# A scheduled two-layer recurrent kernel: new durations in its scheduling model, and a new order of all work

## Chip, cores and metric

The kernel runs on one core of a Trainium2 chip. The metric is the device time in microseconds (us); lower is better. Every kernel here ran several times and was compared with the kernel before on the same chip in the same rounds. A difference under 2% counts as "same", so most questions below, which are about 5 to 50 us in 1590, are answered by the intervals and by the traces.

## The reference, cut to what matters

Two memory-augmented attention layers and two gated feed-forward layers alternate. An attention layer goes through 64 segments of 32 rows one after the other; eight memory rows that a segment puts out are read by the next one, so each layer is a chain of 64 steps.

```python
def _A_ref(x, mem0, Wq, Wk, Wv, Wo, seg_len):      # 16 heads of 256, 8 memory rows
    mem = mem0
    for s in range(n_seg):                          # 64 segments of 32 rows
        h = concat([mem, x[:, 32*s : 32*s+32]])     # 40 rows
        p = softmax(mask(q(h) @ k(h).T / 16))
        o = (p @ v(h)) @ Wo
        mem = o[:, :8]                              # the next segment reads this
        outs.append(o[:, 8:])
def _B_ref(x, W_gate, W_up, W_down):                # width 448 -> 1792 -> 448
    return (relu(x @ W_gate) * (x @ W_up)) @ W_down

x = x + _A_ref(_layernorm(x), ...)
x = x + _B_ref(_layernorm(x), ...)
x = x + _A_ref(_layernorm(x), ...)                  # the same weights again
return x + _B_ref(_layernorm(x), ...)
```

## The kernel before

The kernel does not write its instructions in a fixed order. It lists several thousand operations with what they read and write, their engine and a duration in ns, and a greedy list scheduler plays them on model engines. At each point it takes, of the operations that could start about now, the one with the highest priority: the length of the longest chain behind it, plus a constant from a fitted table. The order in which the model starts operations is the order in which the program issues them. **So a duration in the model never changes how long anything takes on the chip. It changes the order alone.**

```python
BIAS = { "": 86257.0, "t_block": 36012.0, ... , "stay": 41740.0 }     # fitted priorities, cut

class _Order:
    LAT = {"pe": 170.0, "act": 0.0, "dve": 0.0, "pool": 60.0, "sp": 2200.0}
    def run(self):
        ...                                    # t: when o could start on engine e (inputs, buffers, engine)
        lim = max(f, t0) + (60.0 if e == "pe" else 40.0)
        stay = BIAS.get("stay", 0.0) if e == "pe" else 0.0
        t, o = max((x for x in lst if x[0] <= lim), key=lambda x: (x[1].prio + stay * (x[1].mode == mode), -x[0]))
        ...
        c = o.cost[e]
        if e == "pe" and o.mode != mode:
            c += 95.0                          # a change of TensorE's tile form
        if e in ("act", "dve"):
            free[e] = t + c - 60.0             # back-to-back work overlaps
        ...
    def emit(self):
        for o in self.order:                   # what the model started first is issued first
            ...

@staticmethod
def acost(n):                                  # ScalarE, n columns
    return 186.0 + n / 1.2

def tdma(self, name, out, src, rd, wr):        # small transposes: xAT, xBT, PTs
    self.q.add("dma", ("sp",), {"sp": 1250.0}, lambda E: E.dma_start_transpose(out=out(), in_=src()), rd, wr, name=name, lat=1150.0)
```

Three operations:

- `xBT`: one DMA transpose for each two segments. It turns the layer-normed rows `xn` for the feed-forward layer, which starts with it. In front of it stand `un` (28 or 56 matmuls with `U`, the tile `big` in the trace) and the layernorm.
- `PTs`: one DMA transpose in each segment. It turns the probabilities `Ps` for the products that give `U`.
- `un_mem` and `m_t`: the chain of the memory. 56 matmuls give the eight rows, ScalarE copies their high half (`hi`), VectorE takes the low half (`lo`), selector matmuls (`selm`) transpose both, VectorE copies the result (`hT`), and the next step can begin.

```python
def un_mem(self, t):
    ...
    S.mm(mms, 14 * S.pitch(D) + 100.0, [("UTm", w, 0), ("UTm", w, 1), ...], C.res() + [("hi",), ("lo",)], mode=2)
    S.act(lambda E: E.activation(S.hi[:, :], C.b()[:, 0:D], ACT.Copy), D, C.res(), [("hi",)])
    S.dve(lambda E: E.tensor_tensor(S.lo[:, :], C.b()[:, 0:D], S.hi[:, :], ALU.subtract), D, C.res() + [("hi",)], [("lo",)])

def ln_b(self, p):
    S.ln(S.XB[:, p % 2, :], ...)
    ...
    S.tdma("xBT", lambda: S.xBT[:, :, :], lambda: S.xn[:, 1, :], [("xn", 1, 0), ("xn", 1, 1)], [("xBT",)])
```

Of the kernel before, what the change touches and what calls it, by code (L numbers as in the profile page):

```python
# [12 lines left out]
D = 448  # L13
# [31 lines left out]
class _Sched:  # L45
# [107 lines left out]
BIAS = {  # L153
    "": 86257.0, "t_block": 36012.0, "t_block@a": 23035.0, "t_block+": -1249.0, "s_mem": 20903.0, "s_mem@a": 89077.0,
    "s_mem+": -30020.0, "p_t_mem": 19749.0, "p_t_mem@a": 43910.0, "p_t_mem+": 2707.0, "u_mem": 55095.0,
    "u_mem@a": -130.0, "u_mem+": -99280.0, "un_mem": -459.0, "un_mem@a": 122.0, "un_mem+": -17548.0, "m_t": 272938.0,
    "m_t@a": -12858.0, "m_t+": 2514.0, "s_seg": -17721.0, "s_seg@a": -110875.0, "s_seg+": -84825.0, "seg_pt+": 2945.0,
    "seg_pt@a": 61065.0, "u_seg": -7984.0, "u_seg@a": -190957.0, "u_seg+": -15770.0, "m_nat": 209021.0,
    "m_nat@a": -66163.0, "m_nat+": -6349.0, "ln_a+": 6133.0, "ln_a@a": -40396.0, "un": -45873.0, "un@a": 985.0,
    "un+": -360.0, "ln_b+": 36834.0, "ln_b@a": -3899.0, "b_layer": -14517.0, "b_layer@a": -4185.0,  # L160
    "b_layer+": -36139.0, "b_down": -43343.0, "b_down@a": 11698.0, "ln_a@1": -121626.0, "ln_a@3": 37724.0,
    "m_nat@0": 28359.0, "t_block@0": -6404.0, "s_mem@0": -40022.0, "p_t_mem@0": 40772.0, "u_mem@0": 21364.0,
    "un_mem@0": -28.0, "m_t@0": 7217.0, "s_seg@0": -22838.0, "seg_pt@0": 25164.0, "u_seg@0": -13177.0,
    "m_nat@1": -44414.0, "t_block@1": -40812.0, "s_mem@1": -35149.0, "p_t_mem@1": -28287.0, "u_mem@1": 7776.0,
    "un_mem@1": 2809.0, "m_t@1": 54215.0, "s_seg@1": 31420.0, "seg_pt@1": -53190.0, "u_seg@1": -95775.0,
    "un@1": -60698.0, "ln_b@1": -25.0, "b_layer@1": 856.0, "b_down@1": 23582.0, "m_nat@2": 22936.0,
    "t_block@2": 15930.0, "s_mem@2": 4217.0, "p_t_mem@2": 3111.0, "un_mem@2": 14654.0, "m_t@2": -8423.0,
    "s_seg@2": -46451.0, "seg_pt@2": -6344.0, "u_seg@2": 11507.0, "m_nat@3": -2248.0, "t_block@3": -11479.0,
    "s_mem@3": 20866.0, "p_t_mem@3": -27588.0, "u_mem@3": -4646.0, "un_mem@3": -42313.0, "m_t@3": -49036.0,
    "s_seg@3": 46995.0, "seg_pt@3": -43622.0, "u_seg@3": -33517.0, "un@3": -2265.0, "ln_b@3": -37800.0,  # L170
    "b_layer@3": 13857.0, "b_down@3": 21581.0, "ln_a@z": -7346.0, "m_nat@z": 106537.0, "t_block@z": -39111.0,
    "s_mem@z": 58604.0, "p_t_mem@z": -24682.0, "u_mem@z": -56380.0, "un_mem@z": 22265.0, "m_t@z": -2445.0,
    "s_seg@z": -22084.0, "seg_pt@z": -582.0, "u_seg@z": 1373.0, "un@z": -36250.0, "ln_b@z": 47261.0,
    "b_layer@z": -69964.0, "b_down@z": -85774.0, "seg_pt": 19866.0, "ln_b": 14929.0, "stay": 41740.0,
}
# [26 lines left out]
class _Order:  # L202
# [70 lines left out]
    def run(self):  # L273
        self.graph()
        free = {e: 0.0 for e in self.ENGS}
        mode = 0
# [10 lines left out]
        while len(order) < total:  # L287
            best = None
            for e in self.ENGS:
                f = free[e]  # L290
                lst = []
                for o in cand[e]:
                    t = f
                    for q in o.preds:
                        h = self.hop(q.fixed, e)
                        x = q.fin + h if h >= 0 else 0.0
                        if x > t:
                            t = x
                    if o.alloc:
# [4 lines left out]
                        if x > t:  # L304
                            t = x
# [3 lines left out]
                    for r in bk:  # L309
                        for src, x in bankt.get(r, {}).items():  # L310
                            if src != e and x + 35.0 > t:
                                t = x + 35.0
# [32 lines left out]
            if e in ("act", "dve"):  # L345
                free[e] = t + c - 60.0
            else:
                free[e] = t + c
# [60 lines left out]
class _Kernel:  # L409
# [133 lines left out]
    def setup(self):  # L543
# [18 lines left out]
        def load_t(w, q):  # L562
            S.q.add("dma", ("sp",), {"sp": 3600.0}, lambda E: E.dma_start_transpose(out=st[w, q], in_=src[w][:, q * 1024:(q + 1) * 1024]),
                    (), [(w, q)], name=f"{w}{q}", lat=2500.0)

        def load_o(q, wr=()):
            S.q.add("dma", ("sp",), {"sp": 3000.0}, lambda E: E.dma_start(st["Wo", q], S.Wo_d[:, q * 8:q * 8 + 8, :]),
                    (), [("Wo", q)] + list(wr), name=f"Wo{q}", lat=2500.0)

# [114 lines left out]
        for h, W, d, n in ((0, S.Wg, S.Wg_d, "Wg"), (1, S.Wu, S.Wu_d, "Wu")):  # L684
            S.q.add("dma", ("sp",), {"sp": 5000.0}, lambda E, W=W, d=d: E.dma_start(W, d[0:384, :].rearrange("(k p) c -> p k c", p=128)),
                    (), where[n] + [(n,)], name=n, lat=2500.0)
            S.q.add("dma", ("sp",), {"sp": 800.0}, lambda E, h=h, d=d: E.dma_start(S.W3[64 * h:64 * h + 64, :], d[384:448, :]),
                    (), where["Wg"] + [("W3", h)], name=f"W3{h}", lat=2500.0)
        S.q.add("dma", ("sp",), {"sp": 6000.0}, lambda E: E.dma_start(S.Wd, S.Wd_d.rearrange("(c p) d -> p c d", p=128)), (),
                where["Wd"] + [("Wd",)], name="Wd", lat=2500.0)  # L690
        S.stage = [("Wv", 3), ("Wo", 0)]
# [23 lines left out]
    @staticmethod  # L715
    def acost(n):
        return 186.0 + n / 1.2

# [97 lines left out]
    def tdma(self, name, out, src, rd, wr):  # L816

        self.q.add("dma", ("sp",), {"sp": 1250.0}, lambda E: E.dma_start_transpose(out=out(), in_=src()), rd, wr, name=name, lat=1150.0)

# [157 lines left out]
    def u_mem(self, t):  # L977
        S = self
        pp, s = (t // 2) % 2, t % 2
        l0, l1 = S.layers(t)  # L980
        C = {l: S.tile("R", 1) for l in range(l0, l1)}
        S.mm(lambda: [m for c in range(4) for l in range(l0, l1) for m in S.u_mms(l, c, pp, s, C[l].b()[:, c * 128:], S.PTm, 8)], 335.0,
             [("PTm",)] + [("hKx", pp, s, l) for l in range(l0, l1)] + [("hKm", pp, s, l) for l in range(l0, l1)],
             [r for l in C for r in C[l].res()] + [("UTm", S.win(t), l) for l in C], mode=1, mode2=3)
        for l in range(l0, l1):
            a = 48 * S.win(t) + 8 * l
            S.cp(lambda a=a: S.UTm[:, :, a:a + 8], lambda l=l: C[l].b()[:, 0:D].rearrange("p (o q) -> p o q", o=NO), D,
                 C[l].res(), [("UTm", S.win(t), l)], eng=("act", "dve") if l1 - l0 == 1 else (("act", "dve")[l],))

    def un_mem(self, t):  # L990
# [12 lines left out]

        S.mm(mms, 14 * S.pitch(D) + 100.0, [("UTm", w, 0), ("UTm", w, 1)] + [("UW", c) for c in range(4)] + (S.Nkeys if t == 0 else []), C.res() + [("hi",), ("lo",)], mode=2)
        S.act(lambda E: E.activation(S.hi[:, :], C.b()[:, 0:D], ACT.Copy), D, C.res(), [("hi",)])
# [53 lines left out]
    def u_seg(self, t):  # L1059
# [3 lines left out]
        for c in range(4):  # L1063
# [3 lines left out]
            for l in R:  # L1067
                home, k = S.home(t, l)
                key[l] = home, k + (c,)
            S.mm(lambda c=c, R=R: [m for l in range(l0, l1) for m in S.u_mms(l, c, pp, s, R[l].b(), S.PTs, SEG)],  # L1070
                 S.pitch(512) + 12.0 if c < 3 else S.pitch(256) + 30.0,
                 [("PTs",)] + [("hKx", pp, s, l) for l in range(l0, l1)] + [("hKm", pp, s, l) for l in range(l0, l1)],
# [189 lines left out]
```

## Time and profile before

| | before |
|---|---|
| time, median (range) | 1589.8 us (1588.0 to 1590.8) |
| span of the profiled run, granted TensorE clock | 1589.0 us, 0.993 |
| TensorE busy | 1511.9 us, 95% |
| TensorE instructions | 30146 matmuls, as many weight loads |

TensorE is the bound, so the profile is read by what it waits for. This is the table of TensorE's waits over the whole run of the kernel before (total us, times, longest us; "..." are rows of the start-up and others).

```profile
PE b L128 <- DVE big L732: 18.1, 31, 1.2
PE b L128 <- DMA xBT<-xn: 15.8, 17, 1.5
...
PE b L128 <- DMA PTs<-Ps: 5.2, 11, 0.7
PE b L128 <- DVE lo L1006: 4.6, 11, 1.5
PE b L128 <- DVE hT L732: 2.1, 4, 0.8
```

Two rows name a transpose, 21.0 us together. The rows with `lo` and `hT` are the chain of the memory.

The columns of a timeline are start us, length us, engine, operation; a bracket names idle time before the line.

```profile
729.77 2.83 PE L128 MATMUL b<-Nw,UTm 128*32 128x448 bf16 x56
732.54 0.82 PE L128 MATMUL b<-PTs,hK 40*128 40x512 bf16 x6
733.29 0.95 PE L128 MATMUL b<-Nw,big 128*64 128x448 bf16 x8
734.17 0.30 PE L128 MATMUL b<-PTs,hK 40*64 40x256 bf16 x4
734.40 0.18 PE L128 MATMUL b<-selm,hi 128*128 128x16 bf16 x1
...
735.63 0.27 PE L128 MATMUL b<-hT,Mw 128*128 128x80 bf16 x3 [0.47 <-DVE big L732]
```

`un_mem` runs from 729.77. Its result needs until 734.4 to become `hi` and `lo`. TensorE fills that time with matmuls of `PTs` and with eight of `un` (`Nw,big`, 0.95 us), and the selector matmuls find `lo` ready: no bracket.

### The profile page before, as it was taken

To read this page: it belongs to the slowest core of one execution; us is meant where nothing else is said; L and a number is where in the kernel's file an instruction comes from. 1 tells how busy PE (TensorE), PEld (TensorE's weight loads), DVE (VectorE), ACT (ScalarE), POOL (GpSimd) and SP (SyncE) were. 2 spreads that over 40 slices of the span, in tenths; PEclk is the share of its full clock that TensorE was granted. 3 is DMA by queue.
4 is the path that set the end of the run, shared out by engine and by line. 5 is a ranking of instruction groups with operands and counts; after the bars stand their busy time and mean duration, and the time that the engine had idled before them with its cause. 6 is when DMAs were issued, how large, how long until landed. Compare 5 with 4: busy or idle time off the path is not lost. (4 is left out here: it accounts for less than half of the span.)

```text
span 1589.0 us, 67167 instructions
## 1 busy us (share of the span) xinstructions
PE 1511.9 (95%) x30146; PEld 1079.9 (68%) x30146; DVE 1074.0 (68%) x2893; ACT 706.5 (44%) x2059; POOL 112.4 (7%) x259
## 2 busy tenths in 40 slices
PE   5989999999999999999999999999999999999998
PEld 2556677767766677667766776776667677666775
DVE  8745767676666767676676767666676766767664
ACT  5523544445343444444343444535344443534443
POOL 4000000000000000000000000000000000000000
PEclk9989999999999999999999999999999999999999
DMA  9911100000000010000000101101000000000010
GB/s 213 254 47 21 17 17 16 19 19 16 14 19 16 17 16 19 19 18 15 16 19 14 19 15 19 15 14 19 14 19 16 18 16 14 17 14 17 14 21 13
DMA packets 128654, 45.05 MB, mean 28 GB/s; under 512 B 117480, under 2 KB 127472, under 8 KB 128368
## 3 DMA queue, kind: packets, MB, share of 16 engines
q1 hardware_dynamic: 128016, 40.52, 12.4%
q8 instruction: 238, 3.90, 1.1%
q14 instruction: 48, 0.39, 0.1%
q10 hardware_dynamic: 352, 0.24, 0.1%
HBM read 10.33 MB, written 1.84 MB: 8 GB/s over the span
## 5 line engine op out<-in xcount | busy, mean ns | idle before, releaser
L128 PE MATMUL b<-hT,Mw 128*128 128x80 bf16 (+1 forms) x11424 | 442.9, 200 | 12.1 <-DVE big L732 7.1
L128 PEld LDWEIGHTS b<-hT,Mw 128*128 128x128 bf16 x11424 | 419.9, 100 | 39.5 <-DVE big L732 13.3
L128 PE MATMUL b<-Nw,big 128*64 128x448 bf16 (+1 forms) x1936 | 309.0, 356 | 11.0 <-DVE big L732 10.2
L128 PE MATMUL b<-xBT,big 128*128 128x128 bf16 (+3 forms) x3920 | 203.9, 215 | 17.3 <-DMA xBT<-xn 15.8
L128 PEld LDWEIGHTS b<-Nw,big 128*64 128x64 bf16 (+1 forms) x1936 | 126.1, 104 | 128.1 <-issue 22.7
L732 DVE CAST TTs<-b 128x320 bf16<-128x320 f32 (+5 forms) x420 | 189.5, 451 | 30.6 <-PE b L128 29.6
L731 ACT ACTIVATE TTm<-b 128x80 bf16<-128x80 f32 (+5 forms) x416 | 95.4, 229 | 257.2 <-PE b L128 256.1
L731 ACT ACTIVATE TTs<-b 128x384 bf16<-128x384 f32 (+4 forms) x464 | 193.0, 416 | 35.5 <-PE b L128 29.4
L128 PEld LDWEIGHTS b<-xBT,big 128*128 128x128 bf16 (+1 forms) x3920 | 178.8, 97 | 41.4 <-DMA xBT<-xn 18.0
L128 PE MATMUL b<-Nw,UTm 128*32 128x448 bf16 x3752 | 191.9, 356 | 0.8 <-ACT UTm L731 0.6
L732 DVE CAST big<-b 128x512 bf16<-128x512 f32 (+1 forms) x192 | 117.0, 617 | 90.1 <-PE b L128 86.1
L732 DVE CAST TTm<-b 128x80 bf16<-128x80 f32 (+4 forms) x468 | 107.4, 229 | 96.9 <-PE b L128 91.7
L128 PEld LDWEIGHTS b<-Nw,UTm 128*32 128x32 bf16 x3752 | 97.3, 97 | 86.0 <-ACT UTm L731 12.3
L731 ACT ACTIVATE UTm<-b 128x512 bf16<-128x512 f32 (+2 forms) x174 | 91.0, 541 | 127.3 <-PE b L128 126.8
L128 PE MATMUL b<-hT,M 64*128 64x80 bf16 (+3 forms) x3808 | 141.7, 197 | 1.3 <-DVE hT L732 1.3
L732 POOL COPY hK<-xn 32x448 bf16<-32x448 bf16 x136 | 75.2, 553 | 715.4 <-DVE xn L769 709.1
L128 PEld LDWEIGHTS b<-hT,M 64*128 64x128 bf16 (+1 forms) x3808 | 106.5, 97 | 20.7 <-DVE hT L732 7.5
L731 ACT ACTIVATE big<-b 128x512 bf16<-128x512 f32 (+1 forms) x196 | 96.8, 551 | 36.6 <-PE b L128 36.2
L128 PE MATMUL b<-big,hB 128*128 128x448 bf16 (+1 forms) x490 | 98.9, 354 | 0.2 <-DVE hB L1162 0.2
L1161 ACT ACTIVATE gT<-b 128x512 bf16<-128x512 f32 (+2 forms) x128 | 69.3, 542 | 59.0 <-PE b L128 58.7
L1162 DVE TENSOR_TENSOR hB<-gT,b 128x512 bf16<-128x512 bf16 (+2 forms) x128 | 79.2, 619 | 20.8 <-PE b L128 16.2
L128 PE MATMUL b<-PTs,hK 40*128 40x512 bf16 (+1 forms) x640 | 81.4, 343 | 6.3 <-DMA PTs<-Ps 5.2
(112 smaller groups left out, 1529.9 us busy)
## 6 DMA issues: line engine op xcount, KB each, us to landing
big<-in_A_Wo_dram SPq DMA_DIRECT2D x3, 896.0 KB, 5.6
out_dram<-ys SPq DMA_DIRECT2D x32, 56.0 KB, 1.9
big<-in_B_W_down_dram SPq DMA_DIRECT2D x1, 1568.0 KB, 7.0
XA<-in_A_x_dram SPq DMA_DIRECT2D x28, 56.0 KB, 2.1
big<-in_B_W_up_dram SPq DMA_DIRECT2D x1, 1344.0 KB, 8.1
big<-in_B_W_gate_dram SPq DMA_DIRECT2D x1, 1344.0 KB, 11.9
PTs<-Ps SPq DMA_TRANSPOSE x67, 2.4
Nw<-in_A_Wo_dram SPq DMA_DIRECT2D x1, 896.0 KB, 6.2
```

The costliest lines, as they stand in the source:

```text
L128: ins = E.matmul(out, lhsT=lhsT, rhs=rhs, **kw)
L731: return E.activation(out(), src(), ACT.Copy)
L732: return E.tensor_copy(out(), src())
L1161: S.act(lambda E, g=g, R=R, n=n: E.activation(S.gT[:, g, 0:n], R[0].b()[:, 0:n], ACT.Relu), n, R[0].res(), [("gT", g)])
L1162: S.dve(lambda E, g=g, R=R, n=n, fcs=fcs: E.tensor_tensor(S.hB[:, fcs[0]:fcs[-1] + 1, 0:w], S.gT[:, g, 0:n].rearrange("p (a b) -> p a b", ...
```

## The change

Its intent: the model's durations are set to what traces show, the priorities are fitted again by a search against the new model, and everything is scheduled anew. The small transposes change most, from 1250 + 1150 to 1200 + 2600 ns until they land. No operation is added or taken away.

```diff
 BIAS = {
-    "": 86257.0, "t_block": 36012.0, "t_block@a": 23035.0, "t_block+": -1249.0, "s_mem": 20903.0, "s_mem@a": 89077.0,
+    "": 19808.0, "t_block": 66021.0, "t_block@a": -66472.0, "t_block+": -29034.0, "s_mem": 44979.0,
 ... (the whole table is new; "stay" 41740 -> 60591)
             if e in ("act", "dve"):
-                free[e] = t + c - 60.0
+                free[e] = t + c - (84.0 if e == "dve" else 104.0)
 ... (loads of weights at the start: SyncE 3000 to 6000 -> 500 to 650, landing 2500 -> 3200 to 7000;
      their transposes 3600 -> 4100 or 6200, landing 2500 -> 2900)
     def acost(n):
-        return 186.0 + n / 1.2
+        return 165.0 + n / 1.2
     def tdma(self, name, out, src, rd, wr):
-        self.q.add("dma", ("sp",), {"sp": 1250.0}, ..., name=name, lat=1150.0)
+        self.q.add("dma", ("sp",), {"sp": 1200.0}, ..., name=name, lat=2600.0)
     def un_mem(self, t):
-        S.mm(mms, 14 * S.pitch(D) + 100.0, ...)
+        S.mm(mms, 14 * S.pitch(D) + 20.0, ...)
 ... (two more tails of matmul groups: 335 -> 325, 30 -> 16)
```

## The prediction

> **What bounds the kernel now.** I read the page first: busy shares, then the costliest groups, then the table of waits of TensorE alone, then stretches of the timeline around the longest of those waits, and last the landing times of the three small DMA transposes.
>
> The busy line of the page, and the first stretches of the table by stage (columns: length, then busy us and instruction count of PE, PEld, DVE, ACT, POOL, the granted clock, the DMA share, GB/s):
>
> ```profile
> PE 1511.9 (95%) x30146; PEld 1079.9 (68%) x30146; DVE 1074.0 (68%) x2893; ACT 706.5 (44%) x2059; POOL 112.4 (7%) x259
> ...
> 0.00:40.00 40.00, 22.86 (x121) 9.90 (x122) 32.23 (x112) 20.41 (x69) 18.09 (x30) 1.00 1.08 214
> 40.00:80.00 40.00, 36.42 (x515) 21.18 (x515) 28.56 (x79) 22.75 (x57) 0.53 (x2) 0.99 0.95 256
> 80.00:120.00 40.00, 35.82 (x806) 23.64 (x804) 19.41 (x78) 11.43 (x43) 0.37 (x2) 0.84 0.16 42
> ...
> 400.00:600.00 200.00, 195.63 (x3921) 141.73 (x3918) 135.70 (x357) 88.02 (x255) 11.83 (x29) 1.00 0.09 16
> 1000.00:1200.00 200.00, 190.53 (x3797) 136.69 (x3797) 134.91 (x349) 89.60 (x259) 11.86 (x29) 1.00 0.10 16
> ```
>
> The reader is to see that TensorE is the bound: it is idle only 1589.0 - 1511.9 = 77 us in all, some 25 us of that in the first 120 us, where the DMA engines are full (share 0.95 to 1.08) with the weight loads. VectorE at 68% and ScalarE at 44% have room. A reordering adds and removes no instruction, so it can win only idle time of TensorE and its losses between matmuls. The two 200 us stretches also differ: 4.4 us idle against 9.5 us.
>
> What TensorE waits for between 200 and 1500 us (total us, times, longest):
>
> ```profile
> PE b L128 <- DVE big L732: 16.8, 29, 1.2
> PE b L128 <- DMA xBT<-xn: 14.4, 16, 1.5
> PE b L128 <- DMA PTs<-Ps: 4.8, 10, 0.7
> PE b L128 <- DVE lo L1006: 2.8, 9, 0.3
> ```
>
> These four are 38.8 of 40 us of idle time there. I also took the starts of consecutive matmuls in that stretch apart. Matmuls of one tile form follow one another at columns/2.4 + 2.6 ns (36 ns at 80 columns, 56 at 128, 189 at 448; tiled forms side by side share one such slot). That floor sums to 1162 us of 1298. The rest is 40 us of waits and 96 us at the 842 places where the tile form changes (128x128, 64x128, 40x128, 128x64, 128x32 and so on): 114 ns each.
>
> One xBT wait in the timeline of SyncE and TensorE, and the landing times of two transposes (min, median, max):
>
> ```profile
> 1247.60 1.19 SPq L818 DMA_TRANSPOSE xBT<-xn  x1
> ...
> 1251.89 0.62 PE L128 MATMUL b<-xBT,big 64*128 64x128 bf16 x16 [1.51 <-DMA xBT<-xn]
> ```
> ```profile
> L818 SPq DMA_TRANSPOSE xBT<-xn x34: 1189/1192/2222, 118.5 to 1561.4; - x34
> DMA to landing us min/median/max: 2.4/3.0/4.3
> ```
> ```profile
> L818 SPq DMA_TRANSPOSE PTs<-Ps x67: 1189/1190/2332, 75.2 to 1550.0; - x67
> DMA to landing us min/median/max: 2.4/2.4/9.8
> ```
>
> So an undisturbed transpose lands 2.4 us after its start, exactly the 1250 + 1150 ns that the old model plans for, but some take up to 4.3. I compared each transpose after 150 us with the packets of the instruction queue (238 packets, each 1.1 us in the median): of 33 xBT transposes the 9 with no such packet beside them landed in 2.42 us on average, the 24 with one in 3.44; of PTs, 42 clear ones took 2.49 and 21 with one beside them 3.57. The old order has no room for this lateness.
>
> **What the Trainium skill says.** "Runtime: NRT & Kernel Launch", section Instruction fetch mechanics: an engine's instructions are refilled in blocks of 16 KiB by a DMA queue of the sequencer's own. The trace agrees: 238 packets and 3.90 MB on the instruction queue is 16.4 KB each. "DMA: Bandwidth & Descriptors", section Issuing engines are not separate DMA queues: all DMAs share the 16 engines and interleave; the split of landing times above fits that. "TensorEngine Tiling (Array Packing)", section Key Properties: changing the tiling mode drains TensorE; the trace agrees, 114 ns a change. "ScalarE: Activation LUTs", section What ACT_TABLE_LOAD costs: an ACTIVATE takes 186 ns + 0.833 ns per column, and back-to-back ones overlap by about 93 ns. The trace has 605 ns for 512 columns (the page gives 613) and an overlap of 104 ns in the median of most forms, so the trace's figure is used.
>
> **The change part by part.** No instruction is added or removed; the greedy scheduler gets other durations and a newly fitted table of priorities, and emits another order of the same 30146 matmuls, 2893 VectorE and 2059 ScalarE instructions.
>
> 1. Small transposes: 1200 + 2600 = 3800 ns planned instead of 2400. That gives 1.4 us more lead to xBT, PTs and xAT. The xBT waits (15.8 us in 17 over the whole run, longest 1.5) should nearly all go, since a landing of at most 4.3 leaves 0.5 uncovered: -13 us. PTs (5.2 us in 11, longest 0.7): -4 us.
> 2. Overlap of back-to-back work: 84 ns on VectorE and 104 on ScalarE instead of 60. The trace has 83 and 104, so this is a better fit. A 512-column ScalarE copy now occupies 165 + 427 - 104 = 488 ns in the model instead of 553, where the trace has (2060 - 605)/3 = 485 ns from start to start in a run of four; a VectorE one 599 instead of 623, where the trace has 610. The chip was already that fast, so this wins nothing by itself; it lets the choice between the two engines move copies to ScalarE, which has room, and plans matmuls behind copies at the right time. The waits for copies into the state buffer (VectorE big, 18.1 us in 31 over the run) come partly from late PTs, whose products are those copies, partly from the copy engine chosen. I take a third of them: -6 us. The wait on the low half of the memory state (4.6 us in 11): -1 us.
> 3. TensorE costs: smaller tails in four places (100 to 20, 30 to 16, 335 to 325 ns), and the priority for staying in one tile form rises from 41740 to 60591. Counted over the whole kernel there are 1031 runs of one tile form; if 25 are merged, that is 25 x 114 ns: -3 us.
> 4. Weight loads: SyncE is planned busy for 0.5 to 0.65 us for a plain load instead of 3 to 6, with 5.4 to 7 us to landing; the trace shows 0.37 to 0.65 us and 5.3 to 11.9. Later small DMAs are thus planned behind them properly. But the first 13.5 us of idle wait for setup and for the first rows, and until 60 us the DMA engines are full, so little can come of it: -2 us.
> 5. A new order makes new waits that no table tells me. The periodic pattern of four steps (90.3 us each around 600, 92.6 around 1250) repeats some 16 times, so one new wait of 0.5 us a period is worth 8: +8 us.
>
> Sum: -13 - 4 - 6 - 1 - 3 - 2 + 8 = -21 us, 1589.8 - 21 = 1569 us.
>
> **Rivals.** First: the lead is taken from elsewhere. The layer that waits for xBT also feeds the state that comes back later, and its buffers (eight PSUM banks) are held until copied; planning 1.4 us more latency on 134 transposes could make the chain from Ps over PTs and u_seg to the big copies the limit, and the waits reappear under copies. For it: the wait on copies is already the largest, and the recurrence from step to step is a chain. Against it: VectorE is 68% busy and there is matmul work of other layers to put between; in the good stretch the same kernel idles only 2.2%. It would make 1585 to 1592.
> Second: the search also wins the losses at changes of tile form and nearly all waits. Then up to 35 us of the steady waits, 10 of changes and 5 of the start go, and the time is about 1540. For it: the model now agrees with the trace in nearly every number. Against it: the waits for copies were visible to the old model too, and its search left them there; the order must respect the same dependencies.
> Third: the collisions with instruction fetch shift. Their phase against the four-step period drifts, and the worst stretch (800 to 1370 us) is where they meet xBT. A new order may meet them with PTs instead, or never. With 3.8 us planned this moves the time by some 5 us either way at most.
> Fourth: the clock. It was half for 3.4, 10.2 and 3.4 us between 79 and 138 us, which cost about 8 us; an order with fewer or more holes in the start could save or repeat that: 5 us either way.
>
> **Range and chances.** The sure part is step 1, 17 us; the rest nearly cancels, with the rivals' spread of about 13 us around it. Range 1552 to 1587. Faster by over 2% means under 1558.0, which needs most of the second rival: 0.2. Slower by over 2% would need 32 us of new waits in a loop whose model has become better: 0.02. Within 2%: 0.78.
>
> **What would show it right or wrong.** Step 1: the waits on xBT and PTs, 21 us together, fall under 5 us, with unchanged landing times (2.4 undisturbed). Step 2: the wait on big falls to about 12 us and the share of copies on ScalarE rises over that of before. Step 3: fewer than 1031 runs of one tile form at the same 0.11 us each. Step 4: the first 120 us hold about 23 us of TensorE idle time. The four-step period should come to about 89.5 us and no longer differ between the middle and the late part. Wrong would be: transposes no longer waited for, but the idle sum of TensorE still near 77 us (first rival), or a sum under 45 us (second).

## The result, and the profile after

| | before | after |
|---|---|---|
| time, median (range), 4 runs each | 1589.4 us (1588.0 to 1590.8) | 1591.0 us (1588.8 to 1591.6) |
| ratio after / before, 95% interval | | 1.0007 (0.999 to 1.0025): same |
| profiled run: span, clock | 1589.0, 0.993 | 1586.9, 0.991 |

A ratio in this document is the mean time of one kernel's runs over that of the other's of the same rounds, so it is not quite the ratio of the medians beside it.

The 21 us that were predicted did not come; the time stands outside the range of 1552 to 1587. The busy line after:

```profile
PE 1514.9 (95%) x30146; PEld 1087.2 (69%) x30146; DVE 870.0 (55%) x2303; ACT 861.0 (54%) x2649; POOL 111.0 (7%) x259
```

The same 30146 matmuls, but 590 copies have gone from VectorE (2893 to 2303) to ScalarE (2059 to 2649), and the two are balanced now. TensorE's waits after:

```profile
PE b L128 <- DVE lo L1006: 13.4, 18, 1.5
PE b L128 <- DVE big L732: 10.0, 14, 0.7
...
PE b L128 <- DVE hT L732: 5.6, 16, 0.7
PE b L128 <- DVE UTm L732: 4.9, 15, 0.3
PE b L128 <- DMA PTs<-Ps: 2.3, 4, 0.7
PE b L128 <- ACT big L731: 2.1, 5, 0.8
...
PE b L128 <- DMA xBT<-xn: 0.6, 1, 0.6
```

The two transposes fell from 21.0 to 2.9 us, and the copies into `big` from 18.1 to 12.1. Three rows grew in their place: `lo` from 4.6 to 13.4, `UTm` from 0.6 to 5.7 (0.8 of it behind ScalarE), `hT` behind VectorE by 3.5 (behind all engines from 4.3 to 6.5). All three are links of the memory chain. The counts say where they come from: 15 to 18 times, that is about once in each four steps.

A row names what came last and not the place where TensorE stood, and for `big` that misleads. In the kernel before, 7.1 of its 18.1 us are waits of matmuls that read `hT` (15 times 0.47 us, as in the timeline of before): they stand in the memory chain. Here are the same waits sorted by the matmuls that waited:

| TensorE's waits, us | before | after |
|---|---|---|
| for xBT and PTs, whole run | 21.1 | 2.9 |
| memory chain (readers of `UTm`, `hi`, `lo`, `hT`), 150 to 1500 us | 11.1 | 23.0 |
| `un` and products of `PTs`, nearly all behind copies into `big`, 150 to 1500 us | 11.2 | 11.0 |
| others before 150 us, after 1500 us | 21.2, 2.5 | 21.0, 3.5 |

So by place the copies cost what they had cost: 0.71 us once in four steps, in front of `un` before (the first line) and in front of the products of `PTs` after (the second). The memory chain costs twice as much.

```profile
623.77 0.95 PE L128 MATMUL b<-Nw,big 128*64 128x448 bf16 x8 [0.71 <-DVE big L732]
```
```profile
625.71 0.30 PE L128 MATMUL b<-PTs,hK 40*64 40x256 bf16 x4 [0.71 <-DVE big L732]
```

The timeline of TensorE after, at the same place of the program (the columns are those of the timeline of before):

```profile
642.46 2.83 PE L128 MATMUL b<-Nw,UTm 128*32 128x448 bf16 x56 [0.33 <-DVE UTm L732]
645.22 0.82 PE L128 MATMUL b<-PTs,hK 40*128 40x512 bf16 x6
646.75 0.17 PE L128 MATMUL b<-selm,hi 128*128 128x16 bf16 x1 [0.71 <-DVE lo L1006]
...
648.12 0.28 PE L128 MATMUL b<-hT,Mw 128*128 128x80 bf16 x3 [0.30 <-DVE hT L732]
```

The eight `Nw,big` matmuls between the `PTs` products and the selectors are no longer there. In the new order the last of this `un` ends at 642.13, ahead of `un_mem`, so that the layernorm and the transpose behind it start earlier: `xBT` 3.2 us after the start of `un_mem`, where it was 10.6 us. Nothing is left to cover the chain: 0.33 + 0.71 + 0.30 = 1.34 us of idle time where the old order had 0.47.

The transpose and its first reader at this place:

```profile
645.66 1.19 SPq L818 DMA_TRANSPOSE xBT<-xn  x1
...
655.78 1.40 PE L128 MATMUL b<-xBT,big 64*128 64x128 bf16 x28
```

The reader starts 10.12 us after the transpose, where 3.8 us were planned for it. The other `xBT` of each four steps has 4.28 us there and kept its place. In the kernel before, the two had 2.71 and 2.88 us around 600 to 650 us.

And two stretches of the table by stage (length, then busy us and instruction count of PE, PEld, DVE, ACT, POOL, the clock, the DMA share, GB/s):

```profile
400.00:600.00 200.00, 195.54 (x3905) 142.19 (x3904) 105.19 (x270) 108.77 (x336) 11.94 (x30) 1.00 0.07 15
1000.00:1200.00 200.00, 193.91 (x3907) 141.00 (x3900) 110.88 (x280) 112.17 (x344) 11.66 (x29) 1.00 0.08 17
```

Against the same two rows in the prediction: from 1000 to 1200 TensorE does 3907 matmuls where it did 3797, 3% more, so the stretch where late transposes stood was mended. From 400 to 600 it does 3905 where it did 3921: the stretch that was good before is a little worse.

I then took the starts of consecutive matmuls of the two profiled runs apart as the prediction describes:

| TensorE, whole run, us | before | after | change |
|---|---|---|---|
| floor of the matmuls | 1378.0 | 1378.0 | 0 |
| waits for xBT and PTs | 21.0 | 2.9 | -18.1 |
| waits for copies into big | 18.1 | 12.1 | -6.0 |
| all other waits | 28.1 | 46.6 | +18.5 |
| changes of tile form (1031 and 1030), half clock | 132.4 | 135.4 | +3.0 |

The last row's 3 us are half clock (time in which TensorE was granted half of its clock): the granted clock was half for 23.3 us before and 29.6 us after, and each microsecond of it costs half a microsecond. 10 of the 29.6 are three dips of 3.4 us at 375, 921 and 1286 us; before had none between 140 and 1500. The sum of the changes, -2.6 us, is the change of the span, -2.1, but for rounding and the ends.

The four-step period, from one `un_mem` to the fourth after it, tells the same. In the 13 steady periods before has a least of 89.9 us and a most of 93.1; after has a least of 90.63, which comes up three times, and a most of 92.7. Summed over 13 they are 1187.3 and 1186.5. The new order is steady but its undisturbed pattern is longer.

### The profile page after: what moved, and what is told of

Same layout as the page of the kernel before. It is cut to its first block, busy times and chain, and to the rows that moved or that the text cites. A ratio compares the mean times of both kernels' runs of the same rounds, so it can differ in the third digit from the quotient of the medians. Undisturbed runs are those within 1.5% of the kernel's fastest.

```text
span 1586.9 us, 67069 instructions
## 1 busy us (share of the span) xinstructions
PE 1514.9 (95%) x30146; PEld 1087.2 (69%) x30146; DVE 870.0 (55%) x2303; ACT 861.0 (54%) x2649; POOL 111.0 (7%) x259
## 4 chain that ended last, share of the span: by engine, by line
PE 87%; DVE 7%; ACT 2%; DMA 2%; issue 2%; POOL 0%; DVEq 0%; ACTq 0%; POOLq 0%
PE b L128 87%; DMA PTs<-Ps 2%; DVE lo L1006 1%; ACT hi L1005 1%; DVE stat L762 1%; DVE big L732 1%; DVE xn L769 1%; DVE ys L1185 1%; DVE UTm L732 1%; DVE XA L1177 1%; ACT stat L764 0%; DVE hT L732 0%; DMA xAT<-xn 0%; ACT Mw L731 0%; DVE seln L602 0%
## 5 line engine op out<-in xcount | busy, mean ns | idle before, releaser
L731 ACT ACTIVATE TTs<-b 128x320 bf16<-128x320 f32 (+5 forms) x698 | 297.3, 426 | 34.4 <-PE b L128 33.2
L731 ACT ACTIVATE TTm<-b 128x80 bf16<-128x80 f32 (+5 forms) x698 | 162.6, 233 | 159.4 <-PE b L128 156.2
L128 PE MATMUL b<-xBT,big 128*128 128x128 bf16 (+3 forms) x3920 | 199.3, 214 | 1.1 <-DMA xBT<-xn 0.6
L128 PEld LDWEIGHTS b<-Nw,big 128*64 128x64 bf16 (+1 forms) x1936 | 127.3, 104 | 106.1 <-issue 11.5
L731 ACT ACTIVATE big<-b 128x512 bf16<-128x512 f32 (+1 forms) x259 | 129.0, 567 | 35.5 <-PE b L128 35.3
L732 DVE CAST TTm<-b 64x64 bf16<-64x64 f32 (+4 forms) x186 | 40.1, 216 | 164.0 <-PE b L128 161.9
L732 DVE CAST TTs<-b 64x256 bf16<-64x256 f32 (+4 forms) x186 | 73.1, 393 | 60.4 <-PE b L128 60.3
L731 ACT ACTIVATE UTm<-b 128x448 bf16<-128x448 f32 (+2 forms) x129 | 70.3, 546 | 65.8 <-PE b L128 65.4
L732 DVE CAST UTm<-b 128x448 bf16<-128x448 f32 (+2 forms) x122 | 73.2, 621 | 56.3 <-PE b L128 54.3
L1162 DVE TENSOR_TENSOR hB<-gT,b 128x512 bf16<-128x512 bf16 (+2 forms) x128 | 78.4, 612 | 34.7 <-PE b L128 29.4
L904 DVE TENSOR_REDUCE stat<-b 128x2 f32<-128x80 f32 (+1 forms) x67 | 15.7, 234 | 145.8 <-PE b L128 145.8
```

The lines of the kernel that those rows point to most:

```text
L128: ins = E.matmul(out, lhsT=lhsT, rhs=rhs, **kw)
L731: return E.activation(out(), src(), ACT.Copy)
L732: return E.tensor_copy(out(), src())
L904: S.dve(lambda E: E.tensor_reduce(st[:, 32:32 + nl], src(), AX.X, ALU.max), n, C.res(), [("sm", 0)])
L1162: S.dve(lambda E, g=g, R=R, n=n, fcs=fcs: E.tensor_tensor(S.hB[:, fcs[0]:fcs[-1] + 1, 0:w], S.gT[:, g, 0:n].rearrange("p (a b) -> p a b", ...
```

## Experiments

Two theories at the start. **A: traded.** The lead for the transposes was taken from the memory chain; what the lateness cost before, the chain costs now. **B: other terms ate it** (the clock, the start, or instruction fetch meeting something else), and the lead as such is a gain that could be had beside it. For the third rival of the prediction, that the phase of instruction fetch matters, there are experiments of their own.

Two helpers are estimates of mine, used to choose experiments and to state expectations. A *replay* takes an emitted order and plays it with the changed model's durations and any landing time of the transposes, at 120 ns for a change of tile form. With every transpose on time it gives 1554.0 us for the order before (period 89.61) and 1571.8 for the order after (90.62, where the trace has 90.63). With every one at 3.8 us it gives 1612.8 and 1572.0; with the landing times taken from each trace, 1573.8 and 1573.8. The profiled runs stood 15 and 13 us above these last two, so differences are read from it and not times.

### 1 and 2. Every xBT and PTs late, in both orders

A second transpose of the same source into a scratch tile is issued right ahead of each `xBT` and `PTs`, on the same queue. The wanted one starts 1.2 us later. Results stay correct.

```diff
             elif o.kind == "dma":
+                if o.name in ("xBT", "pts"):
+                    k = self.kern
+                    x = k.xn[:, 1, :] if o.name == "xBT" else k.Ps[:, :, :].rearrange("p a x -> p (a x)")
+                    self.sc.dma("late", (lambda E, x=x: E.dma_start_transpose(out=k.late[:, :, :], in_=x)), res(o.rd), [("late",)], eng=o.fixed)
```

Expected of the order before:

> The order of before, with a dummy transpose of the same shape on the same queue ahead of each xBT and PTs transpose, so that each lands 1.2 us later than it did. Theory A (lateness of these transposes costs the old order time one for one, because it starts their readers 2.7 to 3.6 us after the start of the transpose): the waits for xBT and PTs on TensorE rise from 21 us to over 50, and the time rises by 20 to 45 us, to 1610 to 1635. Theory B (the waits are taken over from waits that would come anyway, so lateness costs little): under 8 us more, below 1598.

Expected of the order after:

> The order of the changed kernel with the same dummy transposes. Theory A: this order leaves 3.7 us or more from the start of a transpose to its reader and lets 1.2 us pass unseen except where an instruction fetch comes on top: 0 to 10 us more, 1590 to 1600. Theory B: as much more as the order of before gets.

Measured: before + late 1643.9 us (ratio 1.0335, 1.0318 to 1.0352); after + late 1622.0 us (1.0184, 1.0152 to 1.0217; its runs spread from 1612.0 to 1624.3, and the profiled one, the fastest, had a granted clock of 0.993 where the others had 0.984 to 0.986). TensorE's waits for transposes in the first and in the second:

```profile
PE b L128 <- DMA xBT<-xn: 48.6, 33, 2.4
PE b L128 <- DMA PTs<-Ps: 18.0, 18, 2.2
```
```profile
PE b L128 <- DMA PTs<-Ps: 25.6, 28, 2.2
...
PE b L128 <- DMA xBT<-xn: 4.0, 4, 1.5
```

In the order before, 33 of the 34 `xBT` are waited for, 48.6 us: it has no room at all. In the order after the same delay makes only 4 of them late, 4.0 us. So the lead that the change bought for `xBT` is real. Both times were above what I expected. In the second, it is `PTs` that fell: its room in the new order was smaller than I had taken it to be, hardly above the 1.2 us that the dummy took.

### 3 and 4. The transpose's planned time alone, in both directions

The prediction's step 1 alone: the old kernel with the new transpose time and nothing else, and the new kernel with the old one. Both keep the priorities that were fitted to the other time.

```diff
-  ... {"sp": 1250.0}, ..., lat=1150.0)      (in the kernel before)
+  ... {"sp": 1200.0}, ..., lat=2600.0)
```
```diff
-  ... {"sp": 1200.0}, ..., lat=2600.0)      (in the changed kernel)
+  ... {"sp": 1250.0}, ..., lat=1150.0)
```

> Before with only the planned times of the small transposes changed (1200 + 2600 ns), old priorities. Theory A: the waits for xBT and PTs fall under 5 us from 21, but the priorities no longer fit the model and waits elsewhere more than take it back: 1605 to 1640. Theory B' (the longer planned latency alone carries the change, priorities matter little): 1585 to 1595.

> The changed kernel with only the planned times of the small transposes put back (1250 + 1150 ns). Theory A: the waits for xBT and PTs come back (over 15 us) and the priorities no longer fit: 1610 to 1650. Theory B': 1585 to 1600, close to before.

Measured: 1625.9 us for the old kernel with the new time (ratio 1.0221, 1.0206 to 1.0236) and 1647.7 us for the new kernel with the old time (1.0366, 1.0347 to 1.0384). The waits of the first:

```profile
PE b L128 <- DVE big L732: 27.1, 56, 0.7
PE b L128 <- DVE UTm L732: 24.0, 27, 1.1
PE b L128 <- DVE lo L1006: 13.6, 32, 1.5
```

`xBT` is not in its list any more and `PTs` has 0.2 us, but `big` rose from 18.1 to 27.1, `UTm` from 0.6 to 24.0, `lo` from 4.6 to 13.6. The trade is the same as in the change, only dearer, since the priorities were not fitted to it. In the second, the waits for transposes came to 6.5 us only, where I expected over 15. Its loss is in `big` (20.5), `UTm` behind ScalarE (11.2), `hT` (10.5) and `TTs` (8.6). Some 20 of its 57 us may be clock, by plain proportion: 0.980 was granted where the kernel before had 0.992 to 0.995. So a priority table belongs to the durations it was fitted with: the new transpose time without the rest of the change loses 2.2%, the rest without it 3.7%. As a test of the size of the trade both are weak, because the misfit is larger than the effect.

### 5, 6 and 7. The phase of instruction fetch

The trace has one 16 KB packet on the instruction queue for each 256 TensorE instructions (a matmul counts as two, with its weight load), one in about 6.7 us. I tabled, for each transpose of before and after, its landing time against the start of the nearest packet. Where the packet starts before the transpose or over 2.3 us after it, most land in 2.4 to 2.6 us; at 0.6 us after, in 3.2 us; at 1.0 to 2.1 us after, most in 3.8 to 4.3 us. The offset of `xBT` in the kernel before drifts from -0.4 us at 200 us of the run through 1 to 2.1 between 1000 and 1340 us. So its lateness should be movable without touching the order: 56 tiny matmuls near the start, behind the first one, shift all later packets by 112 instructions. As a control, 128 of them shift by a whole block of 256, and nothing should move.

```diff
             if o.kind == "pe":
+                npe += 1
+                if npe == 2:
+                    k, b, c = self.kern, self.kern.banks[7], [("ps", 7, 0), ("ps", 7, 1)]
+                    self.sc.pe([MM(b[:, 0:8], k.ident[:, :], k.ident[:, 0:8], start=True, stop=True) for _ in range(56)], [("ident",)], c)
                 self.sc.pe(o.fn(), res(o.rd), res(o.wr))
```

Before, shifted by 56; before, shifted by 128; after, shifted by 56:

> The order of before, with 56 tiny matmuls (112 TensorE instructions) put into TensorE's idle time before 13 us. They move every later 16 KB instruction fetch (one per 256 instructions, one per 6.7 us) about 2.9 us earlier against the same work. Theory A (fetches that fall 0.3 to 2.3 us after the start of a transpose make it late, and in the order of before most xBT transposes sit just there): late xBT transposes fall from 19 to about 10, waits for xBT and PTs from 21 us to under 10, time 1574 to 1584. Theory B (the lateness has another cause, or its waits are taken over by others): 1587 to 1593, waits as before.

> The same with 128 tiny matmuls, 256 instructions, a whole block: the fetches fall where they fell before. Theory A: 1586 to 1593 and waits for xBT and PTs near 21 us. If it also gets faster than 1584, the tiny matmuls themselves and not the phase do it.

> The changed kernel with the 56 tiny matmuls. Theory A: its transposes have 1.2 us of room or more, so the phase does not matter: within 4 us of the changed kernel, 1586 to 1594. Theory B gives the same; a gain of over 8 us would speak for lateness still at work in it.

Measured, beside 1589.3 us for the kernel before on that chip:

| | time, range | ratio (95%) | waits xBT, PTs |
|---|---|---|---|
| before + 56 | 1584.4 (1581.3 to 1585.0) | 0.9967 (0.9955 to 0.9979) | 7.2, 3.5 |
| before + 128 | 1590.4 (1587.0 to 1593.8) | 1.0011 (0.9996 to 1.0025) | 13.8, 4.3 |
| after + 56 | 1588.1 (1583.6 to 1594.8) | 0.9998 (0.9979 to 1.0016) | 1.7, 4.7 |

The shift by half a block halves the `xBT` waits and takes 5 us off the same order; a whole block does nothing. The offsets moved as foretold. The first missed its expectation by a hair on both numbers (1584.35 us; 10.7 us of waits where I had set under 10). The changed order does not care.

### 8. Filling the wait for lo

In the changed kernel, three more matmuls of 448 columns once in each four steps, in the place of the wait for `lo`. They take about the time of that wait. If the gap itself costs clock, as the dips of the half clock in the profile after suggest, filling it is not dearer than leaving it.

```diff
+                if o.cat == "m_t" and o.t % 4 == 2 and 8 <= o.t < 60:
+                    k, c = self.kern, [r for r in res(o.wr) if r[0] == "ps"]
+                    b = k.banks[c[0][1]]
+                    self.sc.pe([MM(b[:, 0:D], k.ident[:, :], k.N[:, 0, :], start=True, stop=True) for _ in range(3)], [("ident",)], c)
```

> The changed kernel with three matmuls of 448 columns (0.57 us, results unused) in the 0.71 us wait for the low half of the memory state, once per four steps. Theory C (clustered waits of TensorE there let its clock fall to half for 3.4 us at a time): mean clock from 0.989 up to 0.993 or more and 1582 to 1588. Theory D (the dips come from elsewhere): clock and time stay, 1589 to 1596.

Measured: 1587.2 us (1584.7 to 1587.9), ratio 0.9986 (0.9973 to 1.0). The wait for `lo` fell from 13.4 to 5.6 us, and the profile has no dip of the clock between 140 and 1500 us. So 39 extra matmuls cost nothing measurable: that time was empty. That the gaps bring the dips about is supported by it and not shown. For it: the kernel of experiment 13 below, which has the same gaps, has four dips in that stretch, and the kernel before has none. Against it: the changed kernel shifted by 56, with its gaps in place, had only one there, and the filled kernel has as much half clock in all as the changed one (29.4 and 29.6 us), at the start and the end.

### 9 and 10. Fetch locked to the period

The drift of the offset can be stopped: six tiny matmuls in each four steps make the instructions of a period a whole number of blocks. The number at the start then sets at which offset `xBT` stays for the whole run. 32 should keep it clear, 64 should put it into the worst place.

```diff
+                npe += 1
+                k, n, b, c = self.kern, 0, self.kern.banks[7], [("ps", 7, 0), ("ps", 7, 1)]
+                if npe == 2:
+                    n = 32                       # 64 in the second kernel
+                elif o.cat == "m_t" and o.t % 4 == 0 and 8 <= o.t < 60:
+                    c = [r for r in res(o.wr) if r[0] == "ps"]
+                    n, b = 6, k.banks[c[0][1]]
+                if n:
+                    self.sc.pe([MM(b[:, 0:8], k.ident[:, :], k.ident[:, 0:8], start=True, stop=True) for _ in range(n)], [("ident",)], c)
```

> The order of before with 32 tiny matmuls before 13 us (64 instructions) and 6 more in every fourth step, so that a four-step period holds nearly a whole number of half fetch blocks and the fetches keep their place against the transposes through the run; this place is one where xBT is clear. Theory A, estimated by replaying the order with the changed model's durations, 120 ns per change of tile form and the landing time by the place of the fetch as measured: at most 6 late xBT, waits for xBT and PTs under 8 us, 1573 to 1582. Theory B (place of the fetch is not the cause): 1588 to 1595.

> The same kernel but with 64 instead of 32 tiny matmuls before 13 us, so that the fetches stay where they make nearly every xBT late. Theory A, same estimate: over 25 late xBT, waits for xBT and PTs over 35 us, 1602 to 1625, although it differs by under 1 us of TensorE work from the one before. Theory B: as b_lock_good, within 5 us.

Measured, beside 1594.0 us for the kernel before on that chip: 1580.8 us with 32 (1578.2 to 1584.3; ratio 0.9922, 0.9906 to 0.9938), and 1620.9 us with 64 (1620.2 to 1623.7; 1.0172, 1.0152 to 1.0192). The waits for `xBT` in the first and in the second:

```profile
PE b L128 <- DMA xBT<-xn: 0.7, 2, 0.4
```
```profile
PE b L128 <- DMA xBT<-xn: 39.0, 30, 1.6
```

Its landing time has a median of 2.4 and a most of 3.3 us in the first, a median of 4.1 and a most of 4.4 in the second, where 30 of 33 are late (over 2.5 us). The first misses its expectation for the waits by a hair (8.1 us with `PTs`, under 8 expected); the other expectations held. The two kernels have the same order and differ by 32 matmuls of 8 columns, under 1 us of TensorE time. They are 40 us apart at the same granted clock (0.995 to 0.998 and 0.995 to 0.996), and the wait for one transpose, 38.3 us more, is nearly all of it. Two things follow. The lateness of `xBT` is caused by where instruction fetch falls. And the order before, with its lateness taken away, runs 13 us faster than it did on the same chip: `xBT` and `PTs` cost 0.7 + 7.4 us here and 15.8 + 5.2 in the profile before, 12.9 less. So the order before is the shorter of the two when its transposes are on time, as the replay said: its ratio to the kernel before is 0.9922 and that of the changed order 1.0007, 13.5 us apart in 1590, where the replay has 18 with every transpose on time.

Not all of these two differences is the order. The six runs with 32 were granted a clock of 0.995 to 0.998, those of the kernel before beside them 0.991 to 0.994, and the changed kernel's 0.989 to 0.991. By plain proportion that is some 5 of the 13 us and up to 10 of the 13.5. Free of the clock are the least periods: 90.03 us here, with six tiny matmuls in each, against 90.63 in the changed order.

### 11. The old durations, fitted again

The kernel before with nothing changed but the priority table. My search fitted it to the old durations but judged each order by replays with the measured durations: one with every transpose on time, three with some of them 1.4 us late.

```diff
 BIAS = {
-    "": 86257.0, "t_block": 36012.0, "t_block@a": 23035.0, "t_block+": -1249.0, "s_mem": 20903.0, "s_mem@a": 89077.0,
+    "": 449715.0, "t_block": 180011.0, "t_block@a": 322306.0, "t_block+": -952951.0, "s_mem": 215610.0, "s_mem@a": 226023.0,
 ... (the whole table; the durations stay)
```

> Before with its old durations (2400 ns for a transpose) but priorities fitted anew by me, judged not by the model's own end but by replays of the order, one with every transpose on time and three with 55% of xBT and PTs late by 0.4 to 1.7 us, at 120 ns per change of tile form. Theory A (room against lateness need not be bought with the blanket 3800 ns, which makes an order that is 18 us longer undisturbed): waits for xBT and PTs under 10 us, other waits not above 50 us, 1574 to 1584. Rival (any order with room pays for it as much as it gains): 1586 to 1594.

Measured: 1579.0 us (1575.8 to 1582.2), ratio to before 0.9908 (0.9892 to 0.9925), so it beats both kernels. Its waits:

```profile
PE b L128 <- DVE big L729: 11.5, 16, 0.8
...
PE b L128 <- DMA xBT<-xn: 5.0, 9, 1.3
PE b L128 <- DMA PTs<-Ps: 4.5, 7, 1.4
```

Its `xBT` land no earlier than before (median 3.2 us, 24 of 33 late), but they are waited for 9 times instead of 17. `lo` has not risen: 1.8 us. `big` is down to 11.5 us by its name alone: the readers of `hT` wait 7.1 us as before, 15 times, now under `part` (the sum that VectorE makes of the result of `un`). By place the memory chain costs 8.9 us (before: 11.1), and the granted clock was that of the kernel before beside it (0.991 to 0.996 and 0.991 to 0.994). So 11.5 of the 21.0 us of waits for the transposes can be won without giving up the memory chain, with 2.4 us planned. The timeline says how: both `xBT` of each four steps have 3.76 us to their readers, and eight matmuls of `un` still stand behind `un_mem`:

```profile
642.26 2.83 PE L128 MATMUL b<-Nw,UTm 128*32 128x448 bf16 x56
645.02 0.82 PE L128 MATMUL b<-PTs,hK 40*128 40x512 bf16 x6
645.77 0.95 PE L128 MATMUL b<-Nw,big 128*64 128x448 bf16 x8
```

### 12 and 13. Is it the 3.8 us as such?

The last question: does planning 3.8 us for each transpose force the long pattern, or another of the new durations, or the luck of one search? The changed kernel, with 1200 + 1200 ns for the transposes and all its other new durations, priorities fitted again by my search for 40 minutes; and the changed kernel with its 1200 + 2600 kept, fitted again by the same search for as long.

```diff
-  ... {"sp": 1200.0}, ..., lat=2600.0)      (the first only)
+  ... {"sp": 1200.0}, ..., lat=1200.0)
 BIAS = {
-    "": 19808.0, "t_block": 66021.0, "t_block@a": -66472.0, "t_block+": -29034.0, "s_mem": 44979.0,
+    "": 238381.0, "t_block": 241466.0, "t_block@a": -7711.0, "t_block+": 15266.0, "s_mem": 370084.0, "s_mem@a": -85047.0,
 ... (whole table; the second kernel has another one)
```

> The changed kernel with the small transposes planned at 1200 + 1200 ns (their undisturbed time) instead of 1200 + 2600, all its other new durations kept, and the priorities fitted again to that model by my search (40 minutes, judged by my replays of the order, a quarter of the weight on time, the rest with some of the transposes 1.4 us late). Theory A (the blanket 3800 ns is what costs the room; the other new durations are harmless): replay 1555 with all transposes on time, 1559 as judged; the replays of the changed kernel and of the first refit stood 19 and 22 us under the chip, so 1576 to 1586, with waits for xBT and PTs back at 5 to 15 us and those for the copies (lo, hT, UTm, big) under 25. Theory B (the other new durations, or the luck of one search, made the changed order long): 1587 to 1595, with waits for copies near the changed kernel's 38.

> Counterpart: the changed kernel with its 1200 + 2600 ns kept and only the priorities fitted again, by the same search for the same 40 minutes from the changed kernel's own priorities. It found 1570 (on time 1569.5, all late 1570.7) where the changed kernel stands at 1572. Theory A: 1585 to 1592, waits for xBT and PTs under 5 us, and those for copies (lo, hT, UTm, big) over 28: with 3800 ns planned for every transpose no search finds the 10 us that the other arm finds. Theory B (luck of the search): it comes out within 3 us of the other arm.

Measured, beside 1592.0 us for the kernel before: the first 1592.0 us (1591.2 to 1595.5; ratio 1.0007, 0.9988 to 1.0025), the second 1586.3 us (1584.9 to 1594.7; 0.9978, 0.9955 to 1.0002). The first is a clear miss: theory A of that text expected 1576 to 1586. The second is what theory A of its text expected. Waits of the first:

```profile
PE b L128 <- DVE hT L729: 11.6, 20, 1.0
PE b L128 <- DVE big L729: 10.8, 15, 0.8
PE b L128 <- DMA xBT<-xn: 9.7, 13, 1.9
```

and, of the second, the selectors in the timeline of TensorE at the place shown before:

```profile
648.86 0.17 PE L128 MATMUL b<-selm,hi 128*128 128x16 bf16 x1 [0.71 <-DVE lo L1003]
```

The second search, from the changed kernel's priorities, stayed in that kernel's pattern to the hundredth: 0.71 us for `lo`, and 0.33 and 0.30 for `UTm` and `hT` beside it as in the changed kernel, least period 90.63. The first has undisturbed periods of 89.7 us, 0.9 us shorter, as before has. Over 13 periods this is worth about 12 us, and it lost them again: 12.7 us of waits for `xBT` and `PTs`, 14.0 us in all for `hT`, of which before has 4.3, and a later start, with the first `un_mem` at 78.9 us of the run where the changed kernel has 71.5. So in this one pair of searches the undisturbed pattern costs with 3.8 us what theory A says, and the whole time does not; one search each does not tell the 3.8 us from the luck of a search. What 1579 us of experiment 11 needs besides 2.4 us planned (its old, longer durations of copies, which leave a margin, or the luck of its search) stays open.

The second also shows how far the clock moves a time: its six runs have 1584.9 to 1586.4 us at a granted clock of 0.991 to 0.995, and 1591.4 and 1594.7 at 0.989 and 0.988. One thousandth of mean clock is 1.6 us by plain proportion. The four runs of the changed kernel beside its first comparison had 0.989 to 0.991, those of before 0.993 in the profiled one.

## Why the prediction was wrong, point by point

**What bounds the kernel** held: TensorE in both kernels, with the same floor of 1378.0 us.

**Step 1, the transposes (-17)** held: 21.0 to 2.9 us, -18.1. `xBT` fell by 15.2, where 13 was said, `PTs` by 2.9 where it was 4. Undisturbed landings stayed at 2.4 us. The lead of `xBT` grew by 7.2 us at one of its two places and by 1.6 at the other, where 1.4 was said for both. For `PTs` the gain may be luck: the shifted changed kernel of experiment 7 waits 4.7 us for it. Experiments 1 and 2 show that the lead of `xBT` is there and what it protects from: 48.6 us of `xBT` waits under the same delay in one order, 4.0 in the other. That instruction fetch is the cause of the lateness, a split of landing times in the prediction, is shown by experiments 5, 6, 9 and 10.

**Step 2, the copies (-6 and -1)**: the number came, the gain did not. The row `big` fell by 6.0, to 12.1 us as foretold, and ScalarE took 590 copies more. But the prediction read the whole row as copies that arrive late for the state buffer, and 7.1 us of it stood at the readers of `hT`; that place now waits 5.3 us under the name of `hT`. By place the copies cost 11.2 us before and 11.0 after, so the agreement is luck. The wait for `lo` rose by 8.8 us instead of falling by 1.

**Step 3, changes of tile form (-3)**: nothing, 1030 runs of one form after 1031.

**Step 4, the start (-2)**: nothing. TensorE was idle for 24.9 us of the first 120 before and for 26.0 after.

**Step 5, the new waits (+8), is the step that failed, and with it the 7 us of step 2.** Step 5 was the only one with no view behind it, half a microsecond a period. Steps 2, 4 and 5 came to -1 us for all waits but those for the transposes; these grew by 12.5 us (18.5 less the 6.0 of `big`), 13.5 more. By place 11.9 of the 12.5 us are the memory chain, 11.1 to 23.0: 0.33 + 0.71 + 0.30 us where 0.47 was, once in a four-step period, at the one place where the chain closes. The rest of the miss is 3 us of tile forms that were not won and 3 us of half clock. That is 13.5 + 3 + 3 = 19.5, less 1.1 that step 1 did better, 18.4: but for rounding and the ends the 18.9 us between the predicted fall of 21 and the 2 us (2.1) by which the profiled span fell.

The first rival had it: "the lead is taken from elsewhere", 1585 to 1592, and 1591.0 came. It named the wrong link (the big copies, whose waits by place stayed) and was right in the rest. What it lacked is the place. To start `xBT` earlier the new order runs all of the `un` in front of it earlier, and `un` was what TensorE did while `hi` and `lo` were made. This much is read from the timelines: the three orders with eight matmuls of `un` behind `un_mem` (before, experiments 11 and 12) have no wait for `lo` there, the orders without them have 0.71 us in most periods (after, experiment 13) or 0.32 us (experiments 3 and 4). Experiment 3 changes the planned time alone, and the eight are gone; experiment 4 plans 2.4 us under the new priorities, and they are gone too. So either half of the change takes them away. No experiment moves these eight alone. That the lead needed this move is not shown, and two numbers speak against it: at this place the order after has 10.12 us where 3.8 were planned, and the order of experiment 11 has 3.76 us and keeps the eight.

And the trade was priced wrongly by the model, not overlooked. My replay of the changed order gives a period of 90.62 us and the chip 90.63, so its gaps were planned. But the new model bills every transpose 3.8 us. Under it the order before costs about 1599 us and the new one 1553, by the kernel's own scheduler: a gain of 46. On the chip a transpose takes 2.4 us unless a packet of instructions meets it, and the lateness that the order before really paid was 21.0 us of waits. The order after pays 0.7 us (by the least periods of the two traces) to 1.0 us (by the replays) in each of 13 steady periods to insure against it. In waits the premium is the 11.9 us of the chain and 1.0 at the end, against 18.1 saved; 3 us of half clock leave the 2 us by which the profiled spans differ.

**The second rival** (1540) is out. **The third** was right in its mechanism and far too small in its size: it said 5 us either way at most with 3.8 us planned, which holds for the changed order (1588.1 and 1591.0), but for the order before the phase of fetch is worth 40 us between the two that were tried. **The fourth** (clock, 5 us either way) fits what is seen, 3 us in the two profiled runs; what brings the dips about is not settled.

**What stays open:** why the search took the order that gives up the cover; whether a better order with 3.8 us planned exists (my search of 40 minutes from the changed kernel found none with a shorter pattern; single moves in the changed order give at most 4 us by replay); and why the fit with all the new durations but 2.4 us for the transposes fell short of the one with the old durations.

## What to carry to other kernels

A scheduling model that bills a transfer its worst landing time can buy a lead at the price of whatever work moves up to make it; before the change, look on the timeline for what that work covers now, and set the price against the waits that the lateness really costs, not against the model's. When a short DMA is late only sometimes, find what meets it, here the fetch of instructions at every 256th of the bound engine, and count the instructions: a few dummies that move the phase can take the lateness away, though such a fix lasts only until the instruction count changes. A row of waits names what came last: before counting on a part of it, look which instructions stood there. A term in a prediction for "new waits" needs the place where the chain closes, read from the trace, or it is a guess that decides the sum.

## What the Trainium skill lacked or had wrong

- "Runtime: NRT & Kernel Launch", Instruction fetch mechanics, puts the cost of crossing a block boundary at one DMA tail bump, "mostly hidden"; no run here isolates that cost on TensorE itself. What the section lacks is that the fetch packet holds up other transfers: a transpose of 2.4 us lands after 3.8 to 4.3 us if the packet starts 1.0 to 2.1 us behind it, and two kernels that differ in that phase alone are 1580.8 and 1620.9 us.
- "DMA: Bandwidth & Descriptors", DMA Transpose (X-bar), gives constraints and no time, and no page that I read has one for this shape. Here a transpose of 128x512 bf16 within SBUF took 2.4 us from its start to its landing undisturbed, in every kernel, with 1.19 us of it on SyncE, and 8 to 10 us for the first `PTs`, near 75 us of the run.
- "ScalarE: Activation LUTs", What ACT_TABLE_LOAD costs, has an overlap of about 93 ns for back-to-back copies on ScalarE; the trace has 103 to 104 in the median.
- The time of one change of tile form: no page that I read gives it; 114 ns, at 842 changes in the steady part of the kernel before.
